# Two score pairs of the next block before the last key tile's values, and splits spread between copies, in an attention kernel with a gated feed-forward network

## The chip, the cores and the metric

The kernel runs on one core of a Trainium2 chip. The metric is device time in microseconds; lower is better. The core's engines work from queues of their own and wait for each other through semaphores: TensorE (PE, with its weight loads shown as PEld), VectorE (DVE), ScalarE (ACT), GpSimd (POOL) and SyncE (SP), which here issues most of the transfers.

## The reference

The kernel takes x (2048 tokens, 512 features), normalises it per token, runs full softmax attention with 32 heads of 16 features on it, and multiplies the result by a gate that a SwiGLU feed-forward network (1792 hidden features) makes from the same normalised tokens. All inputs and the output are float32.

```python
x = A_x
xn = _layernorm(x)
# attention: H = 32, Dh = 16, scale = 16 ** -0.5
q, k, v = heads(xn @ wqkv)
p = softmax(einsum("bhqd,bhkd->bhqk", q, k) * scale)
s = einsum("bhqk,bhkd->bhqd", p, v) merged @ wo
# gate
g = silu((silu(xn @ w_gate) * (xn @ w_up)) @ w_down)
return x + s * g
```

## The kernel before

**Stages.** A prologue (up to about 160 us) normalises x, makes queries, keys and values and parks them in DRAM. The main part interleaves two streams on TensorE. The tail after block 100 projects and gates the last 512 tokens.

**Stream one, attention.** There are 32 *units* (8 groups of 4 heads by 4 query blocks of 512 tokens). A unit goes over 16 key tiles of 128 keys, cut into 3 to 5 *blocks* by the lists `ns` (lines 481 to 496); 101 blocks in all, numbered by `now`. In a block with n key tiles there are 2n *pairs* (a key tile and two heads). The scores of a pair are two matmuls of 50 rows each, one in each half of the array (line 889). Most pairs are *straight* (letter D): they go into one of two PSUM tiles `score[0]`, `score[1]`, and ScalarE takes the exponential of both heads at once (line 905). A few are *copied* (letters A and B, one head each): they go into the one bank `acc[1]`, VectorE copies each half out (lines 917 and 923), and ScalarE takes the exponential in place when the block's straight pairs are done (line 931). Behind all scores of a block come its *values* (function `values`, line 394): for each key tile four heads' products with the probabilities, accumulated in `acc[0]`, four matmuls side by side in 32-column strips. The trace has two matmul records for each of these products, so n tiles give 8n records.

**Stream two, the filling work.** Between the scores run single steps (letter F, `fill`) of generators in a queue: the feed-forward network (`ffn`) and, behind it, the output projection (`project_out`). A step is two matmuls of 64 rows, one in each half of the array, into `bankx` and `banky` (line 186). `events(n, f)` (line 498) writes the order of a block out by hand: two D first, a D about every fourth or fifth step, A and B at planned places, `f` steps in all. `sizes` gives f for each block: 21 or 24 in the feed-forward part, 9 in two blocks and 12 in the last twelve. A block with n = 4 and f = 12 reads `DDFAFFFFDBFFDFFAFDFFDB`, then values.

**The output stage** begins at block `early` = 87. There, two splits of projections for the last query block (9 steps each), then the projections of query blocks 0, 1 and 2 (48 steps each) fill the blocks up to 100. The float32 operands are used as a rounded part and a remainder, so each needs a *split*: a copy (line 293) and a subtraction (line 294) on VectorE. `load_out` (line 306) loads parts of the attention result, `out_splits` (line 342) splits them at the end of a block by a table from block numbers; `ready[b]` counts them, and `blocked()` holds a projection back until it is 4. The finished projections are scaled on VectorE (`whole_out`, lines 357 and 358), then multiplied by the gate and added to x on GpSimd (lines 351 and 352). `gate_rest` (lines 386 and 387) prepares two tiles for the tail in blocks 98 and 99.

**VectorE's order.** `chores` is a list of (cost in steps, work). `run` puts a chore between two copies where the plan has room for its cost, and all that is left (`tidy`) near the block's end. `finish(u)` adds a unit's closing work to it: transpose, reciprocal and scaling (lines 405, 410, 414), for every second group another transpose (430), and at the last group a split (440, 444). It is called through `ends` in the block after the unit's last, behind its second D. `split_hidden` and `split_wd` add the splits for the feed-forward network's second product. All that a block still owes is emitted before its values.

**The loop.** `for now, (u, first, n) in enumerate(blocks)` issues the loads of the next unit's queries (`load_q`, `load_shift`, at a unit's first block), then `run(u, first, n)`. The order of emission is the order on each engine.

Of the kernel before, what the change touches and what calls it, by code (L numbers as in the profile page):

```python
# [19 lines left out]
P = 128  # L20
# [21 lines left out]
EARLY = 2  # L42
PROBS = 12
EPS = 1e-5
FINE = (29, 30)
QSLOT = (0, 1, 0)
KSLOT = (0, 0, 1)

# [2 lines left out]
def tile_block(ctx: ExitStack, tc: tile.TileContext, x, wqkv, wo, w_gate, w_up, w_down, out):  # L51
# [94 lines left out]
    def load_wd(i):  # L146
        raw = one.tile([P, D], F32, tag="wdr", name="wdr")
        sp.dma_start(raw, w_down[(i % NF) * P:(i % NF + 1) * P])
        wdr[i] = raw

    def split_wd(f, i):
        chores.append((2, partial(dve.tensor_copy, wd[:, f, 0], wdr[i])))
        chores.append((3, partial(dve.tensor_sub, wd[:, f, 1], wdr[i], wd[:, f, 0].bitcast(F32))))
# [17 lines left out]
    def split_hidden():  # L171
        while kept:
            f, ga = kept.pop(0)
            chores.append((2, partial(dve.tensor_copy, hh[:, f, 0], ga)))
            chores.append((3, partial(dve.tensor_sub, hh[:, f, 1], ga, hh[:, f, 0].bitcast(F32))))
# [5 lines left out]
    def order():  # L181
        return (1, 0) if lower else (0, 1)
# [30 lines left out]
    def ffn(b):  # L213
        for grp, part in enumerate(GROUPS):
            nf = part.stop - part.start
            for f in range(nf):
                i = b * NF + part.start + f
                if i + 1 < NB * NF:
                    split_gu(i + 1)
                if f:  # L220
                    split_wd(f - 1, i - 1)
                    chores.append((0, partial(load_wd, i)))
                elif i:
                    load_wd(i)
                if i + 2 < NB * NF and i != 1:
                    load_gu(i + 2)
                hi, lo = gu.pop(i)
                n = 0
                for c in range(DC):
                    for wt, j in ((hi, 0), (hi, 1), (lo, 0)):  # L230
                        both(wt[:, c], fx[:, j, c], n == 0, n == 3 * DC - 1)
                        n += 1
                        if n == 3 * DC:
                            th = one.tile([P, TB], F32, tag="th", name="th")
                            ga = two.tile([P, TB], F32, tag="ga", name="ga")
                            act(th, bankx, AF.Tanh, scale=0.5)  # L236
                            dve.scalar_tensor_tensor(ga, th, 1.0, bankx, op0=ALU.add, op1=ALU.mult)  # L237
                            dve.scalar_tensor_tensor(ga, ga, 0.5, banky, op0=ALU.mult, op1=ALU.mult)
                            kept.append((f, ga))
                            if now == 0:  # L240
                                kept.insert(0, first_hidden)
                            if now >= 0:
                                split_hidden()
                            if grp == 1 and f == nf - 1 and b + 1 < NB:
                                load_fx(b + 1, 0)
                                load_fx(b + 1, 1)
                        yield 3 * DC - n
            split_wd(nf - 1, b * NF + part.stop - 1)
            if grp == 1 and b == NB - 1:
                chores.append((0, partial(load_wo, 0)))  # L250
            for t in range(NT):
                n = 0
                for f in range(nf):
                    if t == 0 and f == nf - 1:
                        tidy()
                    for a, w in ((0, 0), (0, 1), (1, 0)):
                        both(hh[:, f, a, t * P:(t + 1) * P], wd[:, f, w], n == 0, n == 3 * nf - 1)
                        n += 1
                        if n == 3 * nf and grp == 0:
                            closing.append(partial(first_half, t))  # L260
                        elif n == 3 * nf:
                            closing.append(partial(second_half, b, t))
                        yield 3 * nf - n
# [57 lines left out]
    ready = [0] * NB  # L321

    def split_out(b, c):
        split_o(lhs[b, c], parts_o[b, c])
        ready[b] += 1

    def out_steps():
        if now == early:
# [11 lines left out]
            load_gate()  # L340

    def out_splits():
        for b, c in {early: ((0, 0), (0, 1)), early + 1: ((0, 2), (1, 0)), early + 2: ((1, 1), (1, 2)),
                     opened[units - 2] + 1: ((2, 0),), opened[units - 2] + 2: ((2, 1),),
                     opened[units - 2] + 3: ((2, 2),)}.get(now, ()):
            split_out(b, c)
        if now - opened[units - 1] - 2 in range(EARLY):
            gate_rest(now - opened[units - 1] - 2)
# [34 lines left out]
            sp.dma_start(last[t], x[r])  # L383

    def gate_rest(t):
        dve.scalar_tensor_tensor(facc[:, t], facc[:, t], 0.5, gate[t], op0=ALU.mult, op1=ALU.mult)
        dve.tensor_add(facc[:, t], facc[:, t], last[t])


    def values(u, kts, probs):  # L390
# [88 lines left out]
    for u in range(units):  # L479
        opened.append(len(blocks))  # L480
        if u == units - 1:
            ns = [4, 3, 3, 3, 3]
        elif u == 0:
            ns = [4, 6, 6]
        elif u in FINE:
            ns = [4] * 4
        elif u == units - 4:
            ns = [5, 4, 4, 3]
        else:
            ns = [5] * 3  # L490
            far = sizes[len(blocks):len(blocks) + 3]
            ns[far.index(max(far)) if far[1] < max(far) else 1] = 6
        kt = 0
        for n in ns:
            blocks.append((u, kt, n))
            kt += n
# [373 lines left out]
    first_hidden = kept.pop(0)  # L870
    ends = []

    def run(u, first, n):
        nonlocal lower
        g, b = divmod(u, NB)
        q = qst[u % 2]
        f = 0 if blocked() or not sizes else sizes.pop(0)
        direct, todo = events(n, f)
        if now == 0:
            for _ in range(4):  # L880
                todo.insert(0, todo.pop(max(i for i, (_, e) in enumerate(todo) if e == "F")))
        pairs = [(kt, j) for kt in range(first, first + n) for j in range(2)]
        straight, copies = pairs[:direct], pairs[direct:]
        probs, waiting = {}, []

        def scores(bank, kt, j, h):
            k, kc = kst[(g * NB + kt // CT) % RING], kt % CT
            r = slice(h * HALF, h * HALF + NROW)
            mm(bank, k[r, j, kc * P:(kc + 1) * P], q[r, j], start=True, stop=True)  # L889

        done = 0
        copying = [t + 1.5 for t, e in todo if e in "AB"]
        final = max(at for at, (_, e) in enumerate(todo) if e == "F")
        free = 0
        for at, (t, e) in enumerate(todo):
            if at == final and not copying:
                tidy()
            if e == "F":
                fill(1)
            elif e == "D":  # L900
                kt, j = straight[done]
                for h in order():
                    scores(score[done % 2][:, h], kt, j, h)
                probs[kt, j] = ppool.tile([P, 2, TB], F32, tag="pr", name="pr")
                act(probs[kt, j], score[done % 2], AF.Exp, scale=0.25)  # L905
                done += 1
                if done == 2:
                    while ends:
                        ends.pop(0)()
                    out_steps()  # L910
            elif e == "A":
                kt, j = copies.pop(0)
                waiting.append((kt, j))
                scores(spare_bank, kt, j, 0)
                lower = True
                probs[kt, j] = ppool.tile([P, 2, TB], F32, tag="pr", name="pr")
                dve.tensor_copy(probs[kt, j][:, 0], spare_bank)  # L917
                free = copying.pop(0) + 3
            else:
                kt, j = waiting[-1]  # L920
                scores(spare_bank, kt, j, 1)
                lower = False
                dve.tensor_copy(probs[kt, j][:, 1], spare_bank)  # L923
                free = copying.pop(0) + 3
            if not copying:
                close()
            while chores and at < final and (not copying or max(free, t) + chores[0][0] <= copying[0] + 0.5):
                free = max(free, t) + chores[0][0]
                chores.pop(0)[1]()  # L929
        for kt, j in waiting:  # L930
            act(probs[kt, j], probs[kt, j], AF.Exp, scale=0.25)  # L931
        tidy()
        out_splits()
        catch_up()
        values(u, range(first, first + n), probs)

    for now, (u, first, n) in enumerate(blocks):
        g, b = divmod(u, NB)
# [101 lines left out]
```

## Time and profile before

| quantity | value |
|---|---|
| runs shown | 1408.77, 1409.44, 1409.55 us; median 1409.44 |
| the profiled execution | 1409.33 us, of which the span is 1407.5 us |
| granted TensorE clock | 0.999 |
| ACT busy | 1081.7 us (77%) |
| DVE busy | 759.2 us (54%) |
| values, line 394 | 4096 records, 465.3 us |
| straight exponentials, line 905 | 858, 1032 ns each |
| copied exponentials, line 931 | 166, 1078 ns each |

Times in the timeline are microseconds from the start of the span. A row gives the start, the time from the first start to the last end, engine, line, operation, output and inputs, shapes and count. Matmuls overlap in the pipeline: two or four that run side by side each show their whole duration, so starts, not durations, give the pace. PE busy time goes on through a wait that falls between two overlapping matmuls.

### The profile page before, as it was taken

To read this page: it belongs to the slowest core of one execution; us is meant where nothing else is said; L and a number is where in the kernel's file an instruction comes from. 1 tells how busy PE (TensorE), PEld (TensorE's weight loads), DVE (VectorE), ACT (ScalarE), POOL (GpSimd) and SP (SyncE) were. 2 spreads that over 40 slices of the span, in tenths; PEclk is the share of its full clock that TensorE was granted. 3 is DMA by queue.
4 is the path that set the end of the run, shared out by engine and by line. 5 is a ranking of instruction groups with operands and counts; after the bars stand their busy time and mean duration, and the time that the engine had idled before them with its cause. 6 is when DMAs were issued, how large, how long until landed. Compare 5 with 4: busy or idle time off the path is not lost.

```text
span 1407.5 us, 27726 instructions
## 1 busy us (share of the span) xinstructions
PE 1398.8 (99%) x11227; PEld 851.8 (61%) x11227; DVE 759.2 (54%) x1287; ACT 1081.7 (77%) x1235; POOL 92.8 (7%) x104
## 2 busy tenths in 40 slices
PE   9999999999999999999999999999999999999998
PEld 7777756555655655565556555655565555555555
DVE  5544455345645553556455645554555446547566
ACT  6733587778788877787888778778887787787885
POOL 4200200000000000000000000000000000000334
PEclk9999999999999999999999999999999999999999
DMA  6778651034544511254524303366224113233333
GB/s 218 262 247 249 181 123 42 13 101 91 123 99 107 127 45 35 51 126 101 136 54 110 91 13 73 84 144 140 65 68 116 41 36 69 64 100 133 119 92 119
DMA packets 126956, 148.17 MB, mean 105 GB/s; under 512 B 12524, under 2 KB 79340, under 8 KB 126052
## 3 DMA queue, kind: packets, MB, share of 16 engines
q1 hardware_dynamic: 121620, 125.79, 35.1%
q0 software_dynamic: 4912, 20.12, 3.8%
q8 instruction: 91, 1.49, 0.5%
q14 instruction: 45, 0.37, 0.1%
q10 hardware_dynamic: 288, 0.39, 0.1%
HBM read 106.68 MB, written 39.58 MB: 104 GB/s over the span
## 4 chain that ended last, share of the span: by engine, by line
PE 87%; DVE 1%; issue 0%; ACT 0%; DVEq 0%
PE acc L394 32%; PE bankx L186 23%; PE score L889 17%; PE banky L186 12%; PE acc L889 3%; PE acc L977 0%; PE banky L977 0%; DVE wd L293 0%; ACT pr L905 0%; DVE wd L294 0%; PE score L977 0%; DVE pr L917 0%; DVE pr L923 0%; DVE y L984 0%; DVE hh L444 0%
## 5 line engine op out<-in xcount | busy, mean ns | idle before, releaser
L905 ACT ACTIVATE pr<-score 128x1024 f32<-128x1024 f32 x858 | 810.9, 1032 | 233.1 <-PE score L889 231.9
L394 PE MATMUL acc<-pr,vst 128*17 128x512 f32 x4096 | 465.3, 593 | 0.0
L889 PE MATMUL score<-qst,kst 50*128 50x512 f32 x1716 | 391.9, 413 | 0.3 <-ACT pr L905 0.3
L186 PE MATMUL bankx<-fx,guh 64*128 64x512 f32 x896 | 333.6, 393 | 0.1
L186 PE MATMUL banky<-fx,guh 64*128 64x512 f32 x896 | 324.5, 392 | 0.0
L394 PEld LDWEIGHTS acc<-pr,vst 128*17 128x17 f32 x4096 | 111.2, 97 | 295.0 <-issue 264.7
L889 PEld LDWEIGHTS score<-qst,kst 50*128 50x128 f32 x1716 | 172.8, 184 | 148.3 <-issue 74.9
L917 DVE COPY pr<-acc 128x512 f32<-128x512 f32 x166 | 114.8, 691 | 181.3 <-PE acc L889 178.7
L186 PE MATMUL bankx<-wd,hh 64*128 64x512 f32 x672 | 199.5, 392 | 0.0
L186 PE MATMUL banky<-wd,hh 64*128 64x512 f32 x672 | 197.6, 392 | 0.0
L186 PEld LDWEIGHTS bankx<-fx,guh 64*128 64x128 f32 x896 | 166.4, 186 | 17.9 <-issue 0.9
L186 PE MATMUL banky<-fx,gul 64*128 64x512 f32 x448 | 175.5, 392 | 0.0
L186 PE MATMUL bankx<-fx,gul 64*128 64x512 f32 x448 | 175.2, 391 | 0.0
L931 ACT ACTIVATE pr<-pr 128x1024 f32<-128x1024 f32 x166 | 170.3, 1078 | 0.0
L186 PEld LDWEIGHTS banky<-fx,guh 64*128 64x128 f32 x896 | 166.3, 186 | 6.3
L923 DVE COPY pr<-acc 128x512 f32<-128x512 f32 x166 | 114.8, 692 | 78.2 <-PE acc L889 65.8
L237 DVE SCALAR_TENSOR_TENSOR ga<-th,bankx 128x512 f32<-128x512 f32 x56 | 38.5, 688 | 178.2 <-ACT th L236 178.1
L889 PE MATMUL acc<-qst,kst 50*128 50x512 f32 x332 | 133.6, 402 | 0.9 <-DVE pr L917 0.8
L186 PEld LDWEIGHTS bankx<-wd,hh 64*128 64x128 f32 x672 | 124.8, 186 | 13.1 <-DVE wd L929 0.8
L186 PEld LDWEIGHTS banky<-wd,hh 64*128 64x128 f32 x672 | 124.3, 186 | 4.2
L186 PEld LDWEIGHTS bankx<-fx,gul 64*128 64x128 f32 x448 | 83.7, 187 | 10.0
L186 PEld LDWEIGHTS banky<-fx,gul 64*128 64x128 f32 x448 | 83.5, 186 | 3.3
(165 smaller groups left out, 1316.4 us busy)
## 6 DMA issues: line engine op xcount, KB each, us to landing
gur<-in_B_w_gate_dram SPq DMA_DIRECT2D x56, 256.0 KB
gur<-in_B_w_up_dram SPq DMA_DIRECT2D x56, 256.0 KB
wdr<-in_B_w_down_dram SPq DMA_DIRECT2D x56, 256.0 KB
kst<-k_d SPq DMA_DIRECT2D x192, 64.0 KB
qst<-q_d SPq DMA_DIRECT2D x192, 64.0 KB
fx<-xt_d SPq DMA_DIRECT2D x24, 512.0 KB
q_d<-parts SPq DMA_DIRECT2D x16, 512.0 KB
k_d<-parts SPq DMA_DIRECT2D x16, 512.0 KB
```

What stands on the lines that cost most here:

```text
L186: mm(banks[i], lhs[halves[i]], rhs[halves[i]], start=start, stop=stop)
L237: dve.scalar_tensor_tensor(ga, th, 1.0, bankx, op0=ALU.add, op1=ALU.mult)
L394: mm(acc[0][h * 32:h * 32 + DH + 1], v[:, kt % CT, h * (DH + 1):(h + 1) * (DH + 1)], probs[kt, h // 2][:, h % 2], start=kt == 0, stop=kt = ...
L889: mm(bank, k[r, j, kc * P:(kc + 1) * P], q[r, j], start=True, stop=True)
L905: act(probs[kt, j], score[done % 2], AF.Exp, scale=0.25)
L917: dve.tensor_copy(probs[kt, j][:, 0], spare_bank)
L923: dve.tensor_copy(probs[kt, j][:, 1], spare_bank)
L931: act(probs[kt, j], probs[kt, j], AF.Exp, scale=0.25)
```

## The change

What it does, by parts:

- `scores` moves out of `run`; `scored(u, slot, kt, j)` issues a straight pair and its exponential; `begin` does that for the first two pairs of the next block and keeps them in `begun`. For each block whose successor has a number from `early` to 100, the values of all key tiles but the last come first, then `begin`, then the values of the last key tile. The next `run` takes the two pairs over, strikes its first two D, and calls the unit's end and `out_steps` at once.
- `split_out` and `gate_rest` append chores with costs instead of issuing their work; past block `early` they are appended at the block's first A, otherwise at its end as before. The table of splits has one split a block (88 to 91) after two in block 87, where it had two in each of 87, 88 and 89.
- Unit 28 (`units - 4`) loses its own division and gets the usual one; unit 29 leaves `FINE` and is divided into 3, 3, 3, 4, 3.
- In the feed-forward network the second tile's `split_hidden` is put off from block 0 to the start of the third tile (`second_hidden`), and at the end of a group the split of the last `wd` rows moves to the second place of `chores`.

```diff
-FINE = (29, 30)
+FINE = (30,)
...
+                if i == 2:
+                    split_hidden()
...
                             if now == 0:
-                                kept.insert(0, first_hidden)
+                                second_hidden = kept.pop(0)
+                                kept.append(first_hidden)
                             if now >= 0:
                                 split_hidden()
+                            if now == 0:
+                                kept.append(second_hidden)
...
             split_wd(nf - 1, b * NF + part.stop - 1)
+            chores[1:1] = [chores.pop(-2), chores.pop()]
...
     def split_out(b, c):
-        split_o(lhs[b, c], parts_o[b, c])
-        ready[b] += 1
+        dst, src = lhs[b, c], parts_o[b, c]
+
+        def rest():
+            dve.tensor_sub(dst[1], src, dst[0].bitcast(F32))
+            ready[b] += 1
+
+        chores.append((2, partial(dve.tensor_copy, dst[0], src)))
+        chores.append((3, rest))
...
-        for b, c in {early: ((0, 0), (0, 1)), early + 1: ((0, 2), (1, 0)), early + 2: ((1, 1), (1, 2)),
+        for b, c in {early: ((0, 0), (0, 1)), early + 1: ((0, 2),), early + 2: ((1, 0),), early + 3: ((1, 1),), early + 4: ((1, 2),),
...
     def gate_rest(t):
-        dve.scalar_tensor_tensor(facc[:, t], facc[:, t], 0.5, gate[t], op0=ALU.mult, op1=ALU.mult)
-        dve.tensor_add(facc[:, t], facc[:, t], last[t])
+        chores.append((3, partial(dve.scalar_tensor_tensor, facc[:, t], facc[:, t], 0.5, gate[t], op0=ALU.mult, op1=ALU.mult)))
+        chores.append((3, partial(dve.tensor_add, facc[:, t], facc[:, t], last[t])))
...
-        elif u == units - 4:
-            ns = [5, 4, 4, 3]
+        elif u == units - 3:
+            ns = [3, 3, 3, 4, 3]
...
+    def scored(u, slot, kt, j):
+        for h in order():
+            scores(u, score[slot][:, h], kt, j, h)
+        pr = ppool.tile([P, 2, TB], F32, tag="pr", name="pr")
+        act(pr, score[slot], AF.Exp, scale=0.25)
+        return pr
+
+    begun = {}
+
+    def begin(u, first, n):
+        for j in range(2):
+            begun[first, j] = scored(u, j, first, j)
...
-        done = 0
+        def unit_end():
+            while ends:
+                ends.pop(0)()
+            out_steps()
+
+        done = len(begun)
+        if done:
+            probs.update(begun)
+            begun.clear()
+            todo = [i for i in todo if i not in ((0, "D"), (1, "D"))]
+            unit_end()
...
             elif e == "A":
+                if now > early and not turned_in:
+                    turned_in.append(now)
+                    out_splits()
...
         tidy()
-        out_splits()
+        if not turned_in:
+            out_splits()
+            tidy()
         catch_up()
-        values(u, range(first, first + n), probs)
+        kts = range(first, first + n)
+        if early <= now + 1 < len(blocks):
+            values(u, kts[:-1], probs)
+            begin(*blocks[now + 1])
+            values(u, kts[-1:], probs)
+        else:
+            values(u, kts, probs)
```

More of the change, by code (lines that the diff above doesn't have):

```diff
@@ L871, in tile_block, with scores @@
     ends = []
+    def scores(u, bank, kt, j, h):
+        k, kc = kst[(u // NB * NB + kt // CT) % RING], kt % CT
+        r = slice(h * HALF, h * HALF + NROW)
+        mm(bank, k[r, j, kc * P:(kc + 1) * P], qst[u % 2][r, j], start=True, stop=True)
+    def scored(u, slot, kt, j):
[8 more added lines that the diff above has]
+            begun[first, j] = scored(u, j, first, j)
     def run(u, first, n):
         nonlocal lower
-        g, b = divmod(u, NB)
-        q = qst[u % 2]
         f = 0 if blocked() or not sizes else sizes.pop(0)
@@ L883, in run @@
         straight, copies = pairs[:direct], pairs[direct:]
[L884 to L889, printed above, removed]
-        done = 0
+        probs, waiting, turned_in = {}, [], []
+        def unit_end():
[8 more added lines that the diff above has]
+            unit_end()
         copying = [t + 1.5 for t, e in todo if e in "AB"]
@@ L900, in run @@
             elif e == "D":
[L901 to L905, printed above, removed]
+                probs[straight[done]] = scored(u, done % 2, *straight[done])
                 done += 1
                 if done == 2:
-                    while ends:
-                        ends.pop(0)()
-                    out_steps()
+                    unit_end()
             elif e == "A":
+                if now > early and not turned_in:
+                    turned_in.append(now)
+                    out_splits()
                 kt, j = copies.pop(0)
                 waiting.append((kt, j))
-                scores(spare_bank, kt, j, 0)
+                scores(u, spare_bank, kt, j, 0)
                 lower = True
@@ L920, in run @@
                 kt, j = waiting[-1]
-                scores(spare_bank, kt, j, 1)
+                scores(u, spare_bank, kt, j, 1)
                 lower = False
```

## The prediction

> **What bounds the kernel now.** I read the page first, then the waits of TensorE, then the timeline around the output stage (blocks 87 to 100 of 101), then a table by stretches.
>
> ```profile
> PE 1398.8 (99%) x11227; PEld 851.8 (61%) x11227; DVE 759.2 (54%) x1287; ACT 1081.7 (77%) x1235; POOL 92.8 (7%) x104
> ...
> L394 PE MATMUL acc<-pr,vst 128*17 128x512 f32 x4096 | 465.3, 593 | 0.0
> ```
>
> TensorE (PE) is "busy" 99%, but an overlapped matmul that waits still counts as busy, so small stalls must be read from start times. The waits name two kinds of them. The first row below is of the matmuls over the whole span, the second of the weight loads in the output stage.
>
> ```profile
> PE acc L889 <- DVE pr L917: 0.8, 2, 0.5
> ```
>
> ```profile
> PEld acc L394 <- ACT pr L931: 7.9, 19, 0.6
> ```
>
> So in the output stage the value products (L394) wait for the last exponentials (L931), and copied scores (L889 into acc) wait for VectorE's copies (L917). Here is the value stage of block 86, where nothing is late, and then the end of block 92 with the start of block 93 (both with four key tiles):
>
> ```profile
> 1270.36 3.63 PE L394 MATMUL acc<-pr,vst 128*17 128x512 f32 x32
> 1273.91 0.73 PE L889 MATMUL score<-qst,kst 50*128 50x512 f32 x4
> ```
>
> ```profile
> 1324.72 0.39 PE L889 MATMUL acc<-qst,kst 50*128 50x512 f32 x1
> 1325.04 4.19 PE L394 MATMUL acc<-pr,vst 128*17 128x512 f32 x32
> 1329.16 0.73 PE L889 MATMUL score<-qst,kst 50*128 50x512 f32 x4
> 1329.73 0.40 PE L186 MATMUL bankx<-fx,wd 64*128 64x512 f32 x1
> ...
> 1329.96 0.39 PE L889 MATMUL acc<-qst,kst 50*128 50x512 f32 x1
> ...
> 1331.21 0.49 PE L889 MATMUL acc<-qst,kst 50*128 50x512 f32 x1
> ```
>
> The same 32 value matmuls take 4.19 us instead of 3.63: 0.56 us of waiting. ScalarE shows for what:
>
> ```profile
> 1320.55 5.70 ACT L905 ACTIVATE pr<-score 128x1024 f32<-128x1024 f32 x6 [1.65 <-PE score L889]
> 1326.13 2.00 ACT L931 ACTIVATE pr<-pr 128x1024 f32<-128x1024 f32 x2
> 1329.76 5.73 ACT L905 ACTIVATE pr<-score 128x1024 f32<-128x1024 f32 x6 [1.62 <-PE score L889]
> ```
>
> Its eight exponentials run back to back until 1328.13, the last tile's values wait for them, and then ScalarE idles 1.62 us until the next block's first scores exist. The period is a ring through both engines. The table by stretches, PE limited to L394 (columns: stretch, length, busy time and count, clock, DMA), gives blocks 73; 84; (85 to 90 left out); 91 to 96; 97 to 100:
>
> ```profile
> 1098.82:1112.47 13.65, 5.34 (x52) 1.00 0.01 1
> 1240.94:1252.88 11.94, 4.48 (x44) 1.00 0.63 191
> ...
> 1310.68:1366.14 55.46, 25.16 (x194) 1.00 0.31 94
> 1366.14:1395.26 29.12, 11.58 (x98) 1.00 0.39 128
> ```
>
> Blocks 91 to 96 take 55.46/6 = 9.24 us each with 25.16/6 = 4.19 of values; blocks 97 to 100 (three tiles) 7.28 each with 2.90 of values. From the start of block 84 to the end of block 100 it is 1395.26 - 1240.94 = 154.32 us, which leaves 154.32 - 11.94 - 55.46 - 29.12 = 57.80 for blocks 85 to 90. This is the budget.
>
> **The change, part by part.**
>
> *Scores between the values.* `begin` issues two score pairs of the next block before the last key tile's values, 14 times (blocks 86 to 99). No arithmetic is added, but TensorE changes twice more per block between score and value shapes. The steps give the price. A step of the projection is 0.23 (1329.73 to 1329.96, where a copied half takes the place of one of two matmuls). Into values: 1324.72 to 1325.04 is 0.32, so 0.09 more. Out of values: 32 matmuls in eight steps of four; the last starts 3.63 - 0.59 = 3.04 after the first, 0.43 per step, and the next score follows at 3.55, 0.08 more than a step. After the change the first two pairs take 0.57 (1329.16 to 1329.73) instead of 0.46: 0.11 more. Sum **0.28 us** per `begin`, 14 x 0.28 = 3.9 us in all. The trace has no value stage of a single tile between two score groups, so I bound this price: below by 0 (a change that is hidden), above by 0.56 (twice the row).
>
> The Trainium skill, "TensorEngine Tiling (Array Packing)", section Key Properties, speaks against this part: it says that changing the tiling mode drains TensorE. "TensorE: Matmul & The Clock Gate", section Single matmul latency, gives some 166 ns for the part of a matmul that overlap hides; as an estimate from it, two drains cost 0.33 per `begin`, 4.6 us in all, and the forecast would be 0.7 us later. The rows above agree with a drain and put it a little lower.
>
> What it gains: the 0.56 of waiting goes where the two score pairs cover it. Check against ScalarE: let T be the start of the early pairs. ScalarE starts them at T + 0.60 (1329.16 to 1329.76) and has them done at T + 2.5 (0.95 each, 5.70/6). The last tile's values start at T + 0.66, the projection at T + 0.66 + 0.43 + 0.51 = T + 1.6, the third pair five and a half steps later, T + 3.0, and ScalarE has it at T + 3.6. Four more plus two copied ones, 3.8 + 2.0, end at T + 9.4 at the latest. The next block's early pairs start at T + 8.96 (below) and its last values at T + 9.6. So the wait is covered, by some 0.2 us only.
>
> Per block: four tiles 9.24 - 0.56 + 0.28 = **8.96**. Three tiles: the values without a wait are 3.63 less two steps (0.87) = 2.76, so only 0.14 of the 2.90 is waiting, and 7.28 - 0.14 + 0.28 = **7.42**: slightly longer than now. Where a three-tile block has 9 steps rather than 12: 7.42 - 0.69 = 6.73.
>
> *Other divisions.* Unit 28 becomes 5, 6, 5 tiles (now 5, 4, 4, 3), unit 29 becomes 3, 3, 3, 4, 3 (now 4, 4, 4, 4). The number of blocks stays 101. Six tiles with 21 steps take 13.65 (block 73), five take 11.94 (block 84), with `begin` behind them 12.22. From block 84 on: 11.94 + 13.65 + 12.22 + 2 x 6.73 (87, 88) + 7.42 (89) + 8.96 (90) + 7.42 (91) + 5 x 8.96 (92 to 96) + 3 x 7.42 (97 to 99) + 7.28 (100) = 149.4. Against 154.3 that is **-4.9 us**. The waits of blocks 87 to 90 are in it: blocks 85 to 90 come to 13.65 + 12.22 + 2 x 6.73 + 7.42 + 8.96 = 55.7 with one tile more than now left to do (block 91 has three instead of four).
>
> *Splits among the copies.* They are now put in one heap behind a block. At the end of block 88 this is so (DVE, then PE):
>
> ```profile
> 1282.25 0.25 DVE L410 RECIPROCAL rl<-o 128x16 f32<-128x16 f32 x1
> ...
> 1283.19 0.42 DVE L414 TENSOR_TENSOR on<-o,rl 128x256 f32<-128x256 f32 x1
> ...
> 1286.85 0.69 DVE L923 COPY pr<-acc 128x512 f32<-128x512 f32 x1 [0.78 <-PE acc L889]
> ...
> 1292.71 0.68 DVE L917 COPY pr<-acc 128x512 f32<-128x512 f32 x1
> ```
>
> ```profile
> 1291.57 0.40 PE L889 MATMUL acc<-qst,kst 50*128 50x512 f32 x1
> ...
> 1293.45 0.49 PE L889 MATMUL acc<-qst,kst 50*128 50x512 f32 x1 [0.32 <-DVE pr L917]
> ```
>
> From L923 to the next L917 VectorE has 5.86 us of work; the second copied half stands 1.88 behind the first, where 1.25 (1329.96 to 1331.21) is usual. The same heap does not vanish: block 87 is now the first of unit 29, so the closing work of unit 28 (L405 to L444), `first_half` and two splits meet in one block of 6.73 us. Its L923 starts some 2.2 us after its first projection step (1.25 between halves, 0.3 before, 0.6 to the copy); 5.86 and the 0.67 of L410 and L414 later, at 8.7, comes the next block's L917. That block's first half is at about 7.1 and its copy could start at 7.6, so the copy is 1.1 to 1.2 late, and TensorE, in order, stands behind the second half with all its projections and scores. I take **+1.2 us** in block 88, with 0 and 1.9 as ends. From block 89 on one split of 1.1 us goes into 7 to 9 us with four copies of 0.69 at most, and I put nothing. This part also moves subtractions away from GpSimd:
>
> ```profile
> 1336.76 1.66 DVE L294 TENSOR_TENSOR hh<-hh 128x512 fp32r<-128x512 f32 x1
> ```
>
> ```profile
> 1336.49 1.39 POOL L351 TENSOR_TENSOR y<-y,gt 128x512 f32<-128x512 f32 x1 [5.35 <-DVE y L358]
> 1337.95 1.62 POOL L352 TENSOR_TENSOR pair<-y,pair 128x512 f32<-128x512 f32 x1
> ```
>
> Beside GpSimd the same subtraction takes 1.66 instead of 0.69. In their new place GpSimd has finished; VectorE was idle behind them, so this is worth nothing on the path.
>
> *The front edits.* The second hidden split leaves block 0's end, where it holds up a copy in block 1; and at a group's end wd's split goes ahead of the remaining chores, which matters only where a unit opens there (blocks 39 and 72).
>
> ```profile
> 172.41 0.40 PE L889 MATMUL acc<-qst,kst 50*128 50x512 f32 x1
> ...
> 174.56 0.47 PE L889 MATMUL acc<-qst,kst 50*128 50x512 f32 x1
> ```
>
> ```profile
> 1093.74 0.18 PEld L186 LDWEIGHTS bankx<-wd,hh 64*128 64x128 f32 x1 [0.41 <-DVE wd L929]
> ```
>
> The halves are 2.15 apart where 1.25 is usual: up to 0.9 to gain; other steps fill part, I take half, 0.45. The load waits 0.41, some of it under the matmul ahead; 0.25 in each of two blocks. Together **-0.95** (0 to -1.7). On SP, `load_q` and `load_shift` (eight transfers) now stand ahead of `load_out` at block 87 and wait there for unit 28's last scores; the splits that need `load_out`'s data come a whole block later, behind the 5.86 us heap, so I put nothing. The early scores themselves need queries that were loaded one unit before.
>
> **Sum.** -4.9 + 1.2 - 0.95 = -4.65. The profiled execution took 1409.33 us (span 1407.5, 1.8 around it), next to the median of 1409.44. So 1409.44 - 4.65 = **1404.8 us**. The ends of block 88's stall (-1.2, +0.7), of the front edits (-0.75, +0.95) and a price of 0 for the switches (-3.9) bound it; with one of the first two at an end it is 1403.6 to 1405.8, with both 1402.9 to 1406.5, with free switches 1400.9.
>
> **Rivals.**
> *The switches cost double.* 0.56 per `begin` adds 3.9: 1408.7, no change. For it: a single tile of values cannot hide its weight loads as four tiles do. Against: the prices above hold at every block.
> *ScalarE stays the bound.* The spare time is only 0.2 us; if the four-tile blocks keep 9.24, six of them give back 0.28: 1406.5, on the edge. For it: third pairs reach ScalarE 1.1 us after it is free. Against: it now idles 1.62 per block.
> *VectorE turns the gain over.* The place is the first copied half of blocks 88 to 91, 93 to 95, 98 and 99: a split or `gate_rest` now stands between two copies, and if GpSimd still holds VectorE the subtraction takes 1.66, and the half behind it with all of TensorE's queue waits. At 1.2 per block, nine blocks give +10.8: 1415.6. It decides from four blocks on that the gain is lost, from seven that the kernel is slower. Against: GpSimd's two operations are over 3.1 us after L358, and the copy comes later than that.
>
> **How the numbers follow.** The forecast's case 0.68, ScalarE 0.10, double switches 0.13, VectorE 0.09. A measurement here tells about 0.2% (2.8 us) from no change, so faster means below 1406.6: 0.68 and 0.06 of the ScalarE case, 0.74; same 0.13 + 0.04 = 0.17; slower 0.09. The range runs from 1401.0 (free switches) to 1409.0 (double ones) and leaves out VectorE's case and what lies past both ends, less than 2 in 10.
>
> **What would show it.** Value stages without the 0.56; four-tile blocks of about 8.96 and three-tile blocks near 7.4 (a loss); ScalarE idle about 1 us before each third pair; a stall of about 1 us at the second copied half of block 88 and nowhere else; L294 back at 0.69. Four-tile blocks still at 9.2, or copied halves late in several blocks, would prove me wrong.

## The result and the profile after

| | before | changed |
|---|---|---|
| median | 1409.13 us (9 runs, 1408.67 to 1409.58) | 1405.18 us (9 runs, 1404.86 to 1405.47) |
| profiled execution, its span | 1409.33 us, 1407.5 | 1405.18 us, 1403.4 |

The ratio is 0.9972, with a 95% interval of 0.9962 to 0.9982: 4.0 us faster. The forecast was 1404.8 us, a gain of 4.65. One run of the experiments (1529.65 us) and one of the kernel before (2109.29), both at a lower granted clock (0.851 and 0.608), are left out of the medians below.

The line numbers have moved: the values are now line 406 (394 before), the scores 888 (889), the straight exponentials 894 (905), the copied ones 961 (931), the copies 947 and 953 (917 and 923), the subtractions of the output splits 333 (294). The engines' busy times on the page hardly differ, since no matmul and no exponential was added or removed (VectorE has four copies more, 336 against 332, from the new divisions):

```profile
PE 1395.8 (99%) x11227; PEld 847.1 (60%) x11227; DVE 753.5 (54%) x1291; ACT 1082.7 (77%) x1235; POOL 90.6 (6%) x104
```

All waits of the matmuls that the profile lists in the whole span of the changed kernel are now in the prologue, four of them with 1.4, 0.7, 0.3 and 0.2 us. The rows for scores that waited for VectorE's copies or for ScalarE are gone. That does not mean that no stall is left, as the starts below show. Here is the end of block 92 with the start of block 93 on TensorE, the same place as in the prediction:

```profile
1321.27 0.40 PE L888 MATMUL acc<-qst,kst 50*128 50x512 f32 x1
1321.60 2.77 PE L406 MATMUL acc<-pr,vst 128*17 128x512 f32 x24
1324.30 0.73 PE L888 MATMUL score<-qst,kst 50*128 50x512 f32 x4
1324.96 1.05 PE L406 MATMUL acc<-pr,vst 128*17 128x512 f32 x8
1325.94 0.50 PE L186 MATMUL bankx<-fx,wd 64*128 64x512 f32 x1
1325.95 0.72 PE L186 MATMUL banky<-fx,wd 64*128 64x512 f32 x2
1326.29 0.39 PE L888 MATMUL acc<-qst,kst 50*128 50x512 f32 x1
```

Three key tiles' values, four score records, one tile's values, then the projection. The 0.56 us of waiting is gone: 24 records take 2.77 and eight take 1.05 from the first start to the last end, which is their pace without a wait. The price is in the starts: early scores and last values take 1325.94 - 1324.30 = 1.64 us where two steps of 0.23 and two of 0.43 would take 1.32. That is 0.32, next to the 0.28 of the prediction. ScalarE, from the last copied exponential of block 92 to the end of block 93:

```profile
1323.65 1.06 ACT L961 ACTIVATE pr<-pr 128x1024 f32<-128x1024 f32 x1
1324.90 1.94 ACT L894 ACTIVATE pr<-score 128x1024 f32<-128x1024 f32 x2 [0.19 <-PE score L888]
1327.93 3.88 ACT L894 ACTIVATE pr<-score 128x1024 f32<-128x1024 f32 x4 [1.09 <-PE score L888]
1331.69 2.00 ACT L961 ACTIVATE pr<-pr 128x1024 f32<-128x1024 f32 x2
```

The idle 1.62 us ahead of a block has become 0.19, and 1.09 stands before the third pair. The last exponential of block 93 ends at 1331.69 + 2.00 = 1333.69. On TensorE the early pairs behind block 93 and its last values follow:

```profile
1333.29 0.73 PE L888 MATMUL score<-qst,kst 50*128 50x512 f32 x4
1333.95 0.62 PE L406 MATMUL acc<-pr,vst 128*17 128x512 f32 x4
```

The last values start at 1333.95: 0.26 to spare, forecast 0.2.

The output stage in one table (TensorE, values alone; stretch, length, busy time and count, clock, DMA). The cuts lie at the first scores of a block, which are now the early pairs: blocks 84; 85; 86; 87; 88; 89; 90 and 91; 92 to 96; 97 to 99; 100.

```profile
1239.93:1251.87 11.94, 4.48 (x44) 1.00 0.62 191
1251.87:1265.55 13.68, 5.35 (x52) 1.00 0.12 40
1265.55:1277.08 11.53, 3.62 (x36) 1.00 0.26 83
1277.08:1284.21 7.13, 2.97 (x28) 1.00 0.93 300
1284.21:1291.40 7.19, 2.97 (x28) 1.00 0.98 349
1291.40:1298.86 7.46, 2.97 (x28) 1.00 0.04 12
1298.86:1315.31 16.45, 6.78 (x60) 1.00 0.31 94
1315.31:1360.27 44.96, 19.11 (x164) 1.00 0.30 99
1360.27:1382.69 22.42, 8.89 (x76) 1.00 0.45 153
1382.69:1391.16 8.47, 3.96 (x36) 1.00 0.09 33
```

A four-tile block takes 44.96/5 = 8.99 us (9.24 before; forecast 8.96), a three-tile block 22.42/3 = 7.47 (7.28 before; forecast 7.42, a loss). From block 84 on the sum is 1391.16 - 1239.93 = 151.23 us against 154.32: 3.09 us gained there. The other 1.01 of the span lies ahead of block 84, which now starts at 1239.93 instead of 1240.94.

### The profile page after: what moved, and what is told of

Same layout as the page of the kernel before. It is cut to its first block, busy times and chain, and to the rows that moved or that the text cites. A ratio compares the mean times of both kernels' runs of the same rounds, so it can differ in the third digit from the quotient of the medians.

```text
span 1403.4 us, 27734 instructions
## 1 busy us (share of the span) xinstructions
PE 1395.8 (99%) x11227; PEld 847.1 (60%) x11227; DVE 753.5 (54%) x1291; ACT 1082.7 (77%) x1235; POOL 90.6 (6%) x104
## 4 chain that ended last, share of the span: by engine, by line
PE 88%; ACT 0%; DVE 0%; issue 0%; DVEq 0%; ACTq 0%
PE acc L406 32%; PE bankx L186 24%; PE score L888 17%; PE banky L186 12%; PE acc L888 3%; PE acc L1015 0%; PE banky L1015 0%; ACT pr L961 0%; ACT pr L894 0%; PE score L1015 0%; DVE y L1022 0%; DVE fx L280 0%; DVE part L300 0%; DVE y L191 0%; DVE pr L947 0%
## 5 line engine op out<-in xcount | busy, mean ns | idle before, releaser
L888 PEld LDWEIGHTS score<-qst,kst 50*128 50x128 f32 x1712 | 176.0, 184 | 147.7 <-issue 67.2
L947 DVE COPY pr<-acc 128x512 f32<-128x512 f32 x168 | 116.2, 691 | 192.5 <-PE acc L888 187.0
```

The source lines that it names most:

```text
L888: mm(bank, k[r, j, kc * P:(kc + 1) * P], qst[u % 2][r, j], start=True, stop=True)
```

## Experiments: one part undone at a time

The first four kernels take one part of the change away and keep the rest.

**Without the early pairs.**

```diff
-        if early <= now + 1 < len(blocks):
+        if False:
```

> The changed kernel without the early pairs; divisions, spread splits and front edits stay. My theory: an early group costs 0.31 us of switching (four score records and one tile of values in the changed trace: 0.66 + 0.98 us against 0.46 + 0.86 without a switch) and pays by the wait it covers. Taken away: six four-tile blocks lose 0.56 - 0.31 = 0.25 each (+1.5), the two nine-step blocks lose 0.70 - 0.31 = 0.39 each (+0.8), five three-tile blocks with 12 steps gain 0.17 each (-0.85), block 86 gains 0.31. In sum +1.1: 1406.3, with value stages of 4.12 us back in blocks 92 to 96 and 2.84 in blocks 97 to 100. Rival, the early pairs carry the whole output stage's gain: +3, 1408. Rival, they only cost: -1 or more, 1404.

Measured: 1406.46 us (11 runs, ratio to before 0.9981, interval 0.9972 to 0.9990), +1.3 against the changed kernel. The value stage of a four-tile block waits again as it did in the kernel before:

```profile
1331.13 0.39 PE L888 MATMUL acc<-qst,kst 50*128 50x512 f32 x1
1331.45 4.21 PE L406 MATMUL acc<-pr,vst 128*17 128x512 f32 x32
1335.59 0.74 PE L888 MATMUL score<-qst,kst 50*128 50x512 f32 x4
```

From the start of block 84 to the end of block 100 the profiled execution is 1.3 longer than that of the changed kernel (152.50 against 151.23). The early pairs are worth about what the balance of wait and price says, and neither rival's time came out.

**With the old divisions.**

```diff
-FINE = (30,)
+FINE = (29, 30)
...
-        elif u == units - 3:
-            ns = [3, 3, 3, 4, 3]
+        elif u == units - 4:
+            ns = [5, 4, 4, 3]
```

> The changed kernel with the old divisions (unit 28 as 5, 4, 4, 3 and unit 29 as 4, 4, 4, 4). My theory, from the lengths in both traces: blocks 84 to 91 would be 11.94 + 10.5 + 10.84 + 6.76 + 8.30 + 3 x 8.99 = 75.3 us, and they are 75.4 in the changed kernel, so the divisions by themselves are worth about 0: 1404.6 to 1405.6, the stall of 0.45 us in block 86 gone. Rival, the shorter blocks are what relieves ScalarE: +1.5 to +2, 1407.

Measured: 1404.89 us (6 runs, 0.9968, 0.9956 to 0.9980), 0.3 below the changed kernel, inside the expected 1404.6 to 1405.6. So the new divisions bring nothing once the early pairs are there. Both kernels have 14 early groups, so the price is the same; the 0.3 is in the output stage (150.90 against 151.23 in the profiled executions), and most of it is the stall of block 86 that is worked out further below.

**With the splits in heaps.** `split_out` and `gate_rest` issue at once at a block's end, two splits in each of blocks 87, 88 and 89.

```diff
-                if now > early and not turned_in:
+                if False:
...
-early + 1: ((0, 2),), early + 2: ((1, 0),), early + 3: ((1, 1),), early + 4: ((1, 2),),
+early + 1: ((0, 2), (1, 0)), early + 2: ((1, 1), (1, 2)),
```

> The changed kernel with the splits issued at once at a block's end again, two in each of blocks 87, 88 and 89, and gate_rest at once. My theory: VectorE comes late to the copies of blocks 89 and 90 as before (0.65 us each, L294 back at 1.6 beside GpSimd), nothing in the later blocks: +1.3, 1406.5. Rival, the spreading is worth nothing because the early pairs give VectorE the time: 1405.2. Rival, the heaps carry most of the gain: +2.5 or more, 1407.7.

Measured: 1406.91 us (11 runs, 0.9983, 0.9974 to 0.9992), +1.7. The profiled execution took 1408.84 us; it starts block 84 at 1242.27, 2.34 later than the changed kernel, and the edit touches nothing ahead of that block, so only the stretch behind it is compared here. VectorE at the end of block 89, then GpSimd, then TensorE in block 90 (line numbers there are 6 lower than in the changed kernel, L941 for L947):

```profile
1301.32 1.70 DVE L300 TENSOR_TENSOR wd<-wd 128x512 fp32r<-128x512 f32 x1
1302.93 1.52 DVE L299 CAST wd<-wd 128x512 fp32r<-128x512 f32 x1
1304.49 0.69 DVE L300 TENSOR_TENSOR wd<-wd 128x512 fp32r<-128x512 f32 x1
1305.10 0.68 DVE L941 COPY pr<-acc 128x512 f32<-128x512 f32 x1
```

```profile
1301.18 1.28 POOL L357 TENSOR_TENSOR y<-y,gt 128x512 f32<-128x512 f32 x1 [20.89 <-ACT pr L955]
1302.54 1.63 POOL L358 TENSOR_TENSOR pair<-y,pair 128x512 f32<-128x512 f32 x1
```

```profile
1303.18 0.39 PE L882 MATMUL acc<-qst,kst 50*128 50x512 f32 x1
...
1305.84 0.49 PE L882 MATMUL acc<-qst,kst 50*128 50x512 f32 x1 [1.09 <-DVE pr L941]
```

Beside GpSimd's two operations a subtraction takes 1.70 and a cast 1.52. The copy starts 1.9 us after its scores, and the second half stands 2.66 behind the first instead of 1.25. The mechanism is as expected, the places are not. From block 84 to block 100 this execution is 1.4 longer (152.61 against 151.23), and that is one stall in block 90, which takes 10.38 instead of 8.99; where the other 0.3 of the +1.7 lies, this execution does not show. Block 89 has no stall: GpSimd was idle for 20.89 us before its first operation here, so nothing held the two splits behind block 88.

**With the old front.** The second hidden split goes back to block 0, and `wd`'s split to the end of the chores.

```diff
-                if i == 2:
-                    split_hidden()
...
-            chores[1:1] = [chores.pop(-2), chores.pop()]
```

> The changed kernel with the old front (second hidden split in block 0, wd's split last at a group's end). My theory: block 84 starts 1.0 us later, as it did before (1240.94 against 1239.93), in steps of 0.5 in block 1 and 0.25 in each of blocks 39 and 72: 1406.2. Rival, the stalls turn up elsewhere and the end does not move: 1405.2.

Measured: 1405.88 us (11 runs, 0.9977, 0.9968 to 0.9986), +0.7. The two blocks with `wd`'s split (39 and 72; TensorE, stretch, length, busy and count, clock, DMA), first in the kernel before, then in the changed one, then with the old front:

```profile
662.93:675.11 12.18, 12.18 (x107) 1.00 1.06 215
1086.64:1098.82 12.18, 12.18 (x107) 1.00 0.30 86
```

```profile
662.42:674.36 11.94, 11.94 (x106) 1.00 1.06 206
1085.91:1097.88 11.97, 11.97 (x107) 1.00 0.31 91
```

```profile
662.57:674.75 12.18, 12.18 (x107) 1.00 1.06 216
1086.23:1098.41 12.18, 12.18 (x106) 1.00 0.32 87
```

0.24 and 0.21, close to the 0.25 each of the prediction. What is left for block 1 is about 0.25 by the medians, less than the 0.45 assumed. Its stall differs between executions: block 1 takes 14.44 us in the profiled execution of the kernel before, 13.96 in that with the old front, which shows no stall there, and 13.93 in that of the changed kernel.

The four parts, undone one at a time, add up to 1.3 - 0.3 + 1.7 + 0.7 = 3.4 of the 4.0 us, so they do not add exactly.

## Experiments: the price and the places of the early pairs

**Nothing but the early pairs**, put on the kernel before.

> The kernel before with nothing but the early pairs (old divisions, heaps and front). My theory: against before, block 86 +0.31, block 87 -0.39, block 88 -0.2, blocks 89 to 96 -0.25 each (-2.0), blocks 97 to 99 +0.17 each (+0.5), VectorE's stalls stay: -1.8, 1407.5. Rival, the early pairs carry the output stage alone: -3, 1406.3. Rival, without the spread splits VectorE's lateness eats them: 0, 1409.3.

Measured: 1407.54 us against 1409.53 for the kernel before, measured beside it (11 and 19 runs; 0.9987, 0.9978 to 0.9996): -2.0, as expected. In the profiled executions the output stage is 1.6 shorter (152.71 against 154.32). VectorE's heaps then still stall blocks 89 and 90, which take 9.77 and 10.05 us where the four-tile blocks behind them take 8.99. So the early pairs alone carry 1.6 to 2.0 of the 4.0 us, and they do not replace the spreading of the splits, which is worth 1.7 beside them.

**28 early groups where there is no wait to cover.**

```diff
-        if early <= now + 1 < len(blocks):
+        if early - 28 <= now + 1 < len(blocks):
```

> The changed kernel with early pairs from block 58 on as well, 28 groups more, in blocks of the feed-forward part whose value stages have no wait to cover (3.56, 4.42 and 5.27 us for four, five and six tiles, 0.03 over the sum of their steps). My theory, 0.31 us each: +8.7, 1413.9. Rival, double price (0.6 each, weight loads of a single tile unhidden): +17, 1422. Rival, the order is free where it does no good: 1405.2. With ScalarE started earlier nothing else should move.

Measured: 1413.65 us (8 runs; 1.0029, 1.0019 to 1.0039): +8.47 for 28, **0.30 us each** (0.29 by the two profiled executions from the start of block 58 to the end of block 100, 494.0 against 485.8 us). On TensorE, in the feed-forward part of this kernel:

```profile
1008.71 0.61 PE L406 MATMUL acc<-pr,vst 128*17 128x512 f32 x4
1009.26 0.72 PE L888 MATMUL score<-qst,kst 50*128 50x512 f32 x4
1009.91 1.05 PE L406 MATMUL acc<-pr,vst 128*17 128x512 f32 x8
1010.89 0.50 PE L186 MATMUL bankx<-fx,guh 64*128 64x512 f32 x1
```

The starts have the same spacing as in the output stage (0.65 and 0.98). The price is paid in full wherever the order is used, and it is not doubled by the single tile.

**Early pairs only where the wait is longer than the price**: not behind blocks 86, 89, 91 and 97 to 99.

```diff
-        if early <= now + 1 < len(blocks):
+        if now >= early and now + 1 < len(blocks) and (n > 3 or now < early + 2):
```

> The changed kernel with early pairs only where the wait is longer than their price: behind blocks 87, 88 and the four-tile ones, not behind 86, 89, 91, 97, 98 and 99. My theory: -0.31 for block 86 and -0.17 for each of the five three-tile blocks, -1.2: 1404.0. Rival: the head start that early pairs give ScalarE is needed by the four-tile block behind a three-tile one, whose value stage then waits again: 1405 or more.

Measured: 1404.61 us (5 runs; 0.9966, 0.9953 to 0.9979): a miss of 0.6. The value stages are as expected, and no four-tile block waits again, so the rival is not the reason either. The loss is in block 87. Copied halves of that block, in this kernel and then in the changed one:

```profile
1278.93 0.39 PE L888 MATMUL acc<-qst,kst 50*128 50x512 f32 x1
...
1280.97 0.50 PE L888 MATMUL acc<-qst,kst 50*128 50x512 f32 x1 [0.50 <-DVE pr L947]
```

```profile
1279.07 0.40 PE L888 MATMUL acc<-qst,kst 50*128 50x512 f32 x1
...
1280.53 0.49 PE L888 MATMUL acc<-qst,kst 50*128 50x512 f32 x1
```

They are 2.04 apart instead of 1.46. The copy of the first half on VectorE and the reciprocal beside it, again in this kernel and then in the changed one:

```profile
1280.12 0.25 DVE L422 RECIPROCAL rl<-o 128x16 f32<-128x16 f32 x1
1280.29 0.63 DVE L947 COPY pr<-acc 128x512 f32<-128x512 f32 x1
```

```profile
1279.82 0.65 DVE L947 COPY pr<-acc 128x512 f32<-128x512 f32 x1
1280.40 0.23 DVE L422 RECIPROCAL rl<-o 128x16 f32<-128x16 f32 x1
```

The copy starts 1.36 after its scores instead of 0.75, and two things make up the 0.61. VectorE enters block 87 with the splits for the first projections (lines 299, 300, 279 and 280) unfinished; counted from the start of block 84 (1240.09 here, 1239.93 in the changed kernel) the scores come 0.30 earlier, since the early group behind block 86 is not paid, and VectorE is no sooner free. And without that group the reciprocal stands ahead of the copy and not behind it, so the copy comes 0.31 later. The next run keeps block 86's group, which undoes both:

```diff
-        if early <= now + 1 < len(blocks):
+        if early <= now + 1 < len(blocks) and (n > 3 or now < early + 2):
```

> The changed kernel with early pairs behind block 86 too, behind 87, 88 and the four-tile blocks, but not behind 89, 91, 97, 98 and 99. In the run without them behind 86, block 87's copied half was late by 0.9 us where the changed kernel has 0.35: VectorE's heap after block 86 then has less time. My theory: block 86's 0.31 is paid back there, and only the five three-tile blocks gain 0.17 each: -0.85 against the changed kernel, 1404.3 to 1404.5, block 87's stretch as in the changed kernel. Rival, the head start does not matter for VectorE: level with the run without (1404.8).

Measured: 1404.32 us (6 runs; 0.9965, 0.9953 to 0.9977), as expected; the order on VectorE is again copy, then reciprocal, and blocks 86 and 87 take 18.67 us together, against 18.92 without the group and 18.66 in the changed kernel. No run changes the order alone, so how the loss divides rests on the times above.

**The choice with the old divisions**, first without and then with the group behind block 86; the diff is that of the old divisions with the conditions above, with `early + 1` for `early + 2`.

> The old divisions with spread splits, the new front, and early pairs behind blocks 87 to 96 only (not behind 86 and 97 to 99). My theory: against the run with old divisions (1404.9) -0.31 and 3 x -0.17: 1404.1, level with the other choice. Rival as there: 1404.9 or more.

Measured: 1404.30 us (5 runs; 0.9964, 0.9951 to 0.9977).

> The old divisions, spread splits, new front, early pairs behind blocks 86 to 96 only. Against the run without those behind 86: +0.31 and -0.15 of VectorE's lateness in block 87: 1404.3 to 1404.6, no difference that can be told from 1404.3. Rival: as with the new divisions, block 86's early pairs pay back more than they cost: 1404.0.

Measured: 1404.36 us (5 runs; 0.9966, 0.9952 to 0.9980). With the old divisions block 86's group makes no difference that can be told, and the rival's 1404.0 did not come. Three kernels lie at 1404.3, some 0.9 below the changed one. Their output stages in the profiled executions (150.16, 150.31 and 150.40 against 151.23) are shorter by about as much. But their runs (1403.82 to 1405.10) and the changed kernel's (1404.86 to 1405.47) overlap a little, and the intervals of the ratios overlap by most of their length, so this is a likely gain and not a proven one.

## Why the prediction was right, step by step

**The wait and its cover.** Right. The 0.56 us was a wait of the last tile's values for ScalarE, and it vanished with ScalarE ahead of need by 0.26. Taking the early pairs away brought it back; adding them alone gave 1.6 to 2.0 of the 4.0 us. The rival of ScalarE falls: four-tile blocks take 8.99 us, not 9.24.

**The price.** Right in kind and slightly low: 0.28 from the boundaries of the old trace, 0.30 by 28 extra groups, 0.32 from the starts above. Three-tile blocks became slower, as forecast. The rival of a double price falls: it asked for +17 where +8.5 came. The Trainium skill's "TensorEngine Tiling (Array Packing)", section Key Properties, says that a change of tiling mode drains TensorE. The 0.30 per two changes agrees with it, and is near the 0.33 that the prediction estimates from the Trainium skill's "TensorE: Matmul & The Clock Gate", section Single matmul latency.

**The divisions.** The prediction summed divisions and early pairs in one table and did not ask what either is worth alone. Beside the early pairs the divisions are worth nothing: 1404.89 without them. What they would be worth without early pairs no run shows.

**VectorE behind block 87.** The term of +1.2 us in block 88 was mis-sized. Blocks 87 and 88 took 7.13 and 7.19 us, 0.86 over 2 x 6.73, where +1.2 was forecast, all of it in block 88. Not all of the 0.86 is VectorE's. With the old divisions there is one three-tile block with nine steps (block 87); it takes 6.92 us and its copied halves are 1.17 apart, where the two blocks here have 1.46 and 1.53. Against that block the late copies cost 7.13 + 7.19 - 2 x 6.92 = 0.48 in both blocks together, and the 6.73 was 0.19 too short for each block, for a reason that no run shows. VectorE in the changed kernel, from block 87's last copy to block 88's first:

```profile
1281.06 0.69 DVE L953 COPY pr<-acc 128x512 f32<-128x512 f32 x1
...
1285.32 0.69 DVE L333 TENSOR_TENSOR hh<-hh 128x512 fp32r<-128x512 f32 x1
...
1287.00 0.68 DVE L947 COPY pr<-acc 128x512 f32<-128x512 f32 x1
```

The heap is 5.94 us and not 5.86 + 0.67: reciprocal and scaling ran ahead of it, between block 87's two copies, where the prediction put them behind the second one. What the step missed is the other end: it let VectorE enter blocks 86 and 87 with nothing owed. Block 86 took 11.53 us up to its early pairs where 11.94 less one tile of 0.86 is 11.08, 0.45 lost. The new divisions put copies into block 86 while VectorE still owes it splits (lines 299, 300, 279 and 280); its first two halves are 1.83 apart. In the run with the old divisions, without copies there, blocks 85 and 86 (up to its early pairs) are:

```profile
1251.86:1262.41 10.55, 10.55 (x94) 1.00 0.15 51
1262.41:1272.05 9.64, 9.64 (x86) 1.00 0.44 137
```

10.55 less a tile of 0.86 is 9.69, so nothing is lost in its block 86. The two errors, 0.34 too much in blocks 87 and 88 and 0.45 not seen in 86, nearly cancelled, and that is luck.

**GpSimd.** All nine subtractions of the output splits are back at 0.68 (groups of line 333; the three figures are minimum, median and longest in ns), as forecast:

```profile
L333 DVE TENSOR_TENSOR hh<-hh x6: 681/682/692, 1285.3 to 1346.6; 128x512 fp32r<-128x512 f32 x6
L333 DVE TENSOR_TENSOR wd<-wd x3: 681/682/682, 1295.9 to 1312.3; 128x512 fp32r<-128x512 f32 x3
```

But "worth nothing on the path" holds for blocks 93 to 95 only: the run with heaps shows that in block 89 the held subtraction and cast make the stall of 1.4 in block 90. The prediction counted that as the waits of blocks 87 to 90 without naming the cause. The rival of VectorE falls: no block from 89 on waits for a copy in the changed kernel.

**The front.** Forecast 0.95, 1.01 between the two profiled executions, 0.7 by undoing it. Blocks 39 and 72 are right to 0.04; block 1 varies between executions, from nothing to 0.5, where 0.45 was taken.

**The sum.** From block 84 on -3.7 was forecast and -3.09 came: block 86 is 0.45 over its term, blocks 87 and 88 0.34 under theirs, and the blocks from 89 on, with the price a little low, are 0.03 to 0.05 over each, 0.5 in all. With the front the span fell by 4.1; that the total is this near the forecast owes something to errors of both signs.

## What to carry to other kernels

A wait at the end of a block can be covered with the next block's first work, but here TensorE paid 0.3 us for each excursion between two shapes, so it belongs where the wait is longer than that. Block 86 with the new divisions shows the limit of that rule: its group covered no wait of TensorE for ScalarE and was still worth its price, for what it did to VectorE's time and order. Busy shares hide such waits: compare the length of the same group of matmuls between a place where nothing is late and the place in question. When an in-order engine owes a heap of work at a block's end, count it into the next block's first copy, also where the block itself seems to have time.

## What the runs showed of the hardware that was not expected

Time saved on one engine can be lost at another: leaving out block 86's early pairs saved TensorE 0.3 us, and the copied half in block 87 came 0.6 later behind the first one, by the times half of it because VectorE was no sooner free for the copy, and half because the reciprocal stood ahead of it. And a cast on VectorE beside GpSimd's elementwise work took 1.52 us instead of 0.42, so that not only subtractions with two operands are held up.
